# Loading two weights ahead of the second batch's raw keys, five conversion steps moved ahead, and the last key-pooling products later, in a pooled-attention and FFN kernel

## The chip, the cores and the metric

The kernel runs on one core of one Trainium2 chip. The metric is the device time of one execution in microseconds (us), the median of several runs; lower is better. The engines are named as the profile names them: PE is TensorE (PEld its weight loads, which overlap PE), DVE is VectorE, ACT is ScalarE, POOL is GpSimd, and SPq is the queue on SyncE that issues transfers.

## The reference

Keys and values are averaged over groups of 8 positions (576 positions become 72), attention runs on those, and its result is the input of a feed-forward network (FFN) with a leaky ReLU. The two weight matrices are float64 arrays, the rest is float32.

```python
B, H, S, D = q.shape                      # 8, 8, 576, 64; pool = 8, scale = 1/8
k_p = k.reshape(B, H, 72, 8, D).mean(axis=3)
v_p = v.reshape(B, H, 72, 8, D).mean(axis=3)
attn = softmax(scale * q @ k_p.T)         # 576 x 72 for each batch and head
x = (attn @ v_p).transpose(0, 2, 1, 3).reshape(4608, 512)
h = x @ w_in                              # 512 -> 2048
out = maximum(0.01 * h, h) @ w_out        # 2048 -> 512
```

## The kernel before

**The FFN** takes x in chunks of 512 tokens, transposed. Its products are made of three matmuls each: a value is split into a high and a low part of a rounded type (`xh` and `xl`, `gh` and `gl`, the two halves of a weight tile `w`), and high times high, high times low and low times high are added up in PSUM. A weight tile is a slice f of 128 of the 2048 hidden columns: `w_in` slice f and `w_out` slice f, 16 of each. `ph` (lines L944 to L946) is the first layer's product of a slice, ACT applies the leaky ReLU (L949) and makes `gh` (L952), DVE makes `gl` (L954), and `acc` (L969 to L971) is the second layer's product.

**The weights** arrive as float64 (512 KB a slice; `stage`, loads at L180 and L184) and are converted on the chip, once. A head of a conversion is two ACT instructions on the raw bits (L202, L203) and three of DVE (L206, L207, L210); its tail is the high part on ACT (L214) and the low part on DVE (L215). The steps are taken in one sequence: head of `w_in` 0, head of `w_in` 1, tail of `w_in` 0, head of `w_out` 0, tail of `w_in` 1, head of `w_in` 2, tail of `w_out` 0, head of `w_out` 1, and so on. `convert_to(n)` takes steps until n are taken; while chunk 0 is multiplied, it is called with 7 + 4f ahead of slice f.

**The attention** of batch 0 runs before the first FFN product, that of batch 1 between the products of chunk 0. Its units are named in `FIRST`: `q` transposes queries (L463, copied to `qT` at L465), `sa`/`sb` make the scores `pss` of four heads (L488), take the row maximum on DVE (L496) and the exponentials `e` on ACT (L500); `au` divides by the sum (`red`, L520, L521) and spreads the result into `at` (L534, L538; on DVE for row tiles 2 and 3 of batch 0, on POOL otherwise); `pu` transposes `at` into `pp` (PE, L591), from which ACT and DVE make `pT_hi`, `pT_rem` (L593, L594, L602), and multiplies it with the values into `pa` (PE, L619, L624); ACT and DVE turn `pa` into `xh` (L636) and `xl` (L637), which frees its bank. In `1kp0` to `1kp3` PE pools the raw keys of batch 1: eight products of `k0raw` ... `k3raw` with the identity each, summed in one bank `pk` (L301). `1kd` moves `pk` into `kT` (L308 on ACT, L309 on DVE). A `c` in `FIRST` is one conversion step.

**What sets the order.** PE runs in exactly the written order, that of `FIRST` and then of the loops. The order on ACT and DVE is set by the scheduler that builds the kernel; it keeps each engine's queue in one fixed order, and an instruction whose input is late holds those behind it. SPq issues the transfers in the order in which they are written. PSUM's banks are handed out in turn: from batch 1 on, attention uses two banks, so `pq` of a row tile needs the bank of a `pa` that `xl` has to have read.

Of the kernel before, what the change touches and what calls it, by code (L numbers as in the profile page):

```python
# [24 lines left out]
def tile_pooled_attention_ffn(  # L25
# [9 lines left out]
    nc = tc.nc  # L35
# [3 lines left out]
    POOL = 8  # L39
    SP = S // POOL  # L40
# [3 lines left out]
    NK = DM // P  # L44
# [18 lines left out]
    ]  # L63
    FIRST = (
# [99 lines left out]
    def spare(f, i, shape, dtype, name):  # L164

        return wts.tile(shape, dtype, tag=f"w{i}_{f}", name=name)

    def stage(f):

        if f >= NF:  # L170
            return
        slot = NF - 1 if f == NF - 2 else NF - 1 - f % SPARE
        for i in range(2):
            shape = [P, DM, 2]
            if slot > f:
                t = spare(slot, i, shape, I32, f"w{i}_bits{f}")
            else:
                t = two.tile(shape, I32, tag="raw", name=f"w{i}_bits{f}")
            if i == 0:
                nc.sync.dma_start(  # L180
                    t.rearrange("p (k f) w -> p k f w", k=NK), w_in[:, :, f * P : (f + 1) * P, :]
                )
            else:
                nc.sync.dma_start(t, w_out[:, f, :, :])  # L184
            bits[i, f] = t

    def convert(i, f):
# [70 lines left out]
    def raw_tile(b, nm):  # L258
        shape = [P, 2, POOL * D]
        if (b, nm) in RAW:  # L260
            return spare(*RAW[b, nm], shape, F32, f"{nm}raw{b}")
        return two.tile(shape, F32, tag="raw", name=f"{nm}raw{b}")
# [21 lines left out]
            )  # L284
        return raw

    def load_pairs(b):

        raws = []
        for p in range(NK):  # L290
            raws.append(raw_tile(b, f"k{p}"))
            raws[p] = raws[p][:SP].rearrange("s x y -> s (x y)").rearrange("s (a i d) -> s a i d", a=POOL, i=2)
            for i in range(2):
                nc.sync.dma_start(
                    raws[p][:, :, i, :], k[b, 2 * p + i].rearrange("(s a) d -> s a d", a=POOL)
                )
        return raws

    def pool_pair(pk, p, raw):
        for a in range(POOL):  # L300
# [375 lines left out]
    def attention(b):  # L676

        st = {}
# [12 lines left out]
            start_v()  # L691
            q_of[b, 3] = load_q(b, 3)

        def keys():
            st["pairs"] = load_pairs(b)

        def values():
            start, st["v"] = load_v(b)
# [91 lines left out]
        def pm(j, g):  # L790
# [3 lines left out]

        return {
            "loads": loads, "keys": keys, "values": values, "lk": lk, "lv": lv, "kd": kd,
            **{f"kp{p}": kp(p) for p in range(NK)}, "ku": ku, "vu": vu, "vp": vp,
            **{f"q{t}": qu(t) for t in range(len(where))},
# [236 lines left out]

    att = [attention(b) for b in range(B)]
    att[0]["loads"]()
    att[1]["keys"]()
    for f in range(SPARE):
        stage(f)  # L1040

    for u in FIRST.split():
        if u == "c":
# [10 lines left out]
    for b in range(2, B):  # L1054
        for j, piece in enumerate(PIECES[b]):
            c = 2 + (2 * TAIL + S * (b - 2) + piece[0][0]) // CH
# [86 lines left out]
```

## Time and profile before

| | us |
|---|---|
| median of 3 runs | 940.96 (940.75 to 941.16) |
| the profiled execution | 941.63 |
| its span | 939.7 |
| PE busy in the span | 907.3 |
| ACT busy | 411.8 |
| DVE busy | 392.3 |
| POOL busy | 176.1 |

The span is what the profiler saw of the program, the time of the execution is 1.9 us longer. Busy times overlap between engines. What PE is not busy, 32.4 us, is the time in which it waits for another engine or a transfer; instructions that run while PE is busy cost nothing of their own.

### The profile page before, as it was taken

The numbers are of one execution on the slowest core, as the hardware profiler recorded it, in microseconds if no ns is written. First come the engines' busy times: TensorE is split into PE (matmuls) and PEld (weight loads), VectorE is DVE, ScalarE is ACT, GpSimd is POOL, SyncE is SP. The second block draws the span as 40 slices with busy tenths as digits, with TensorE's granted clock in tenths as the row PEclk, the third lists the DMA queues.
The fourth block names the chain that finished last, engine by engine and source line by source line (L and its number), as shares of the span: only waits on it lengthen the run. The fifth ranks groups of instructions, "written<-read, shape, count | busy, mean of one in ns | idle before, by whom it ended". The sixth has DMA issues, their size and how long they took to land.

```text
span 939.7 us, 12662 instructions
## 1 busy us (share of the span) xinstructions
PE 907.3 (97%) x4293; PEld 755.8 (80%) x4293; DVE 392.3 (42%) x910; ACT 411.8 (44%) x1304; POOL 176.1 (19%) x329
## 2 busy tenths in 40 slices
PE   4998999999999989999999999999999999999998
PEld 3876788878888868888888888888888888888886
DVE  5799675524343233343244434353335322221111
ACT  4797764535343324343344435443535334223112
POOL 3012110231036520232023112230102001000000
PEclk9899999999999999999999999999999999999999
DMA  9996331242134560753076505840463122101001
GB/s 173 282 241 208 85 93 51 50 112 63 29 91 112 118 112 18 133 83 82 10 124 104 95 22 110 121 73 7 94 86 52 17 62 43 26 1 46 0 1 46
DMA packets 243257, 77.00 MB, mean 82 GB/s; under 512 B 217528, under 2 KB 226744, under 8 KB 243192
## 3 DMA queue, kind: packets, MB, share of 16 engines
q1 hardware_dynamic: 242616, 75.66, 37.6%
q8 instruction: 34, 0.56, 0.2%
q10 hardware_dynamic: 576, 0.52, 0.2%
q14 instruction: 31, 0.25, 0.1%
HBM read 56.56 MB, written 19.60 MB: 81 GB/s over the span
## 4 chain that ended last, share of the span: by engine, by line
PE 78%; DMA 6%; ACT 5%; DVE 3%; SPq 3%; POOL 3%; issue 1%; ACTq 0%; DVEq 0%; POOLq 0%
PE ph L944 12%; PE acc L969 12%; PE ph L946 12%; PE ph L945 12%; PE acc L971 12%; PE acc L970 11%; PE pss L488 3%; SPq L279 2%; DMA vremraw<-in_v_dram 1%; DMA k1raw<-in_k_dram 1%; PE pa L619 1%; ACT e L500 1%; DMA v1raw<-in_v_dram 1%; PE pa L624 1%; ACT w_bits L202 1%
## 5 line engine op out<-in xcount | busy, mean ns | idle before, releaser
L944 PE MATMUL ph<-xh,w 128*128 128x512 f32 x576 | 231.5, 402 | 0.5 <-DVE gl L954 0.5
L969 PE MATMUL acc<-w,gh 128*128 128x512 f32 x576 | 230.3, 400 | 0.0
L946 PE MATMUL ph<-xh,w 128*128 128x512 f32 x576 | 226.0, 392 | 0.6 <-DVE w L215 0.6
L945 PE MATMUL ph<-xl,w 128*128 128x512 f32 x576 | 225.9, 392 | 0.0
L971 PE MATMUL acc<-w,gl 128*128 128x512 f32 x576 | 225.2, 391 | 0.0
L970 PE MATMUL acc<-w,gh 128*128 128x512 f32 x576 | 224.7, 390 | 0.0
L954 DVE TENSOR_TENSOR gl<-ph,gh 128x512 fp32r<-128x512 f32 x144 | 99.0, 688 | 260.6 <-ACT gh L952 260.0
L949 ACT ACTIVATE ph<-ph 128x512 f32<-128x512 f32 x144 | 84.3, 586 | 265.0 <-PE ph L946 265.0
L500 ACT ACTIVATE e<-pss,red 128x72 f32<-128x72 f32 x320 | 98.2, 322 | 94.2 <-DVE red L496 79.8
L946 PEld LDWEIGHTS ph<-xh,w 128*128 128x128 f32 x576 | 108.7, 189 | 24.7 <-DVE w L215 1.0
L971 PEld LDWEIGHTS acc<-w,gl 128*128 128x128 f32 x576 | 108.2, 188 | 23.5
L944 PEld LDWEIGHTS ph<-xh,w 128*128 128x128 f32 x576 | 108.8, 189 | 21.3 <-DVE gl L954 0.9
L945 PEld LDWEIGHTS ph<-xl,w 128*128 128x128 f32 x576 | 108.9, 189 | 20.7 <-DVE xl L637 0.5
L969 PEld LDWEIGHTS acc<-w,gh 128*128 128x128 f32 x576 | 108.3, 188 | 20.8 <-DVE o L1003 0.4
L970 PEld LDWEIGHTS acc<-w,gh 128*128 128x128 f32 x576 | 108.5, 188 | 20.5
L528 POOL TENSOR_TENSOR at<-e,red 128x128 f32<-128x128 f32 x100 | 39.6, 416 | 276.3 <-DVE red L521 103.0
L952 ACT CAST gh<-ph 128x512 fp32r<-128x512 f32 x144 | 84.8, 589 | 3.7
L500 ACT ACTIVATION_READ_ACCUMULATOR e<-pss,red 128x1 f32 x320 | 66.2, 207 | 0.0
L496 DVE TENSOR_REDUCE red<-pss 128x4 f32<-128x288 f32 x80 | 36.2, 453 | 69.2 <-PE pss L488 69.0
L488 PEld LDWEIGHTS pss<-kT,qT 128*128 128x128 f32 x280 | 43.2, 189 | 9.4 <-ACT e L500 2.3
L488 PE MATMUL pss<-kT,qT 128*128 128x144 f32 x280 | 46.0, 286 | 2.6 <-ACT e L500 1.6
L534 POOL TENSOR_TENSOR blocks<-e,red 128x256 f32<-128x256 f32 x24 | 17.6, 732 | 144.6 <-DVE red L521 97.5
(143 smaller groups left out, 805.3 us busy)
## 6 DMA issues: line engine op xcount, KB each, us to landing
w_bits<-in_moe_w_in_dram SPq DMA_DIRECT2D x16, 512.0 KB
w_bits<-in_moe_w_out_dram SPq DMA_DIRECT2D x16, 512.0 KB
out_dram<-o SPq DMA_DIRECT2D x31, 256.0 KB
rows<-at SPq DMA_DIRECT2D x40, 192.0 KB
blocks<-rows SPq DMA_DIRECT2D x40, 120.0 KB
v0raw<-in_v_dram SPq DMA_DIRECT2D x16, 256.0 KB
v1raw<-in_v_dram SPq DMA_DIRECT2D x16, 256.0 KB
blocks<-rows SPq DMA_DIRECT2D x40, 96.0 KB
```

Of the source, the lines that this page charges most:

```text
L488: nc.tensor.matmul(sc[:, 2 * SP * i : 2 * SP * (i + 1)], qT[:, p, :], kT[:, p, :, :].rearrange("d i s -> d (i s)"), start=True, stop=True,)
L500: ins = nc.scalar.activation(e[:, h, :], scv[:, h, :], AF.Exp, bias=mx[:, h : h + 1], accum_out=sm[:, h : h + 1],)
L528: eng.tensor_tensor(cols[:, :, i, :].rearrange("a (h w) y -> a h w y", h=2), e[:, 2 * i : 2 * i + 2, 0:MAIN].rearrange("a h (w y) -> a h w ...
L944: nc.tensor.matmul(ph, w[:, 0, ks], xh[kk], start=kk == 0, stop=False)
L945: nc.tensor.matmul(ph, w[:, 0, ks], xl[kk], start=False, stop=False)
L946: nc.tensor.matmul(ph, w[:, 1, ks], xh[kk], start=False, stop=kk == NK - 1)
L949: nc.scalar.activation(ph, ph, AF.Prelu, alpha=0.01)
L952: casts.append(nc.scalar.copy(gh, ph))
L954: anchor["gl"] = nc.vector.tensor_tensor(gl, ph, gh.bitcast(F32), op=ALU.subtract)
L969: nc.tensor.matmul(a, gh[:, r], hi, start=first, stop=False)
L970: nc.tensor.matmul(a, gh[:, r], lo, start=False, stop=False)
L971: nc.tensor.matmul(a, gl[:, r], hi, start=False, stop=last)
```

## The change

The raw keys' loading is split by pair. The first slice of `w_in` is now issued ahead of the raw keys of batch 1 and the second between the two halves of these keys; the two first slices of `w_out` follow the keys. In `FIRST`, one `c` stands ahead of `au00`, two behind `sa30`, one behind `au01` and the rest late; there are eight in place of seven. `1kp2` moves behind `pu30 pu31`, and `1kp3` from there to behind `au11`, just ahead of `1kd`. The number of instructions on each engine stays the same. In the changed kernel the lines below L297 have numbers that are 4 smaller (L637 becomes L633).

```diff
     FIRST = (
         "k0 q0 sa00 k1 q1 sa01 sa10 sb00 q2 sb01 sa11 lv sb10 sb11 sa20 vu sa21 pu00 pu10 vp q3 "
-        "pu01 pu11 sb20 sb21 au00 sa30 sa31 au01 1kp0 c pu20 pu21 1kp1 sb30 sb31 1kp2 pu30 pu31 1kp3 1kd "
-        "c c au10 c au11 c c c"
+        "pu01 pu11 sb20 sb21 c au00 sa30 c c sa31 au01 1kp0 c pu20 pu21 1kp1 sb30 sb31 pu30 pu31 "
+        "1kp2 c au10 c au11 1kp3 1kd c c"
     )
...
-    def stage(f):
+    def stage(f, which=range(2)):
...
-        for i in range(2):
+        for i in which:
...
-    def load_pairs(b):
-
-        raws = []
-        for p in range(NK):
...
+    def load_pair(b, p):
+
+        raw = raw_tile(b, f"k{p}")
...
+        for i in range(2):
+            nc.sync.dma_start(raw[:, :, i, :], k[b, 2 * p + i].rearrange("(s a) d -> s a d", a=POOL))
+        return raw
...
-        def keys():
-            st["pairs"] = load_pairs(b)
+        def keys(*pairs):
+            st.setdefault("pairs", []).extend(load_pair(b, p) for p in pairs)
...
     att[0]["loads"]()
-    att[1]["keys"]()
+    stage(0, [0])
+    att[1]["keys"](0, 1)
+    stage(1, [0])
+    att[1]["keys"](2, 3)
     for f in range(SPARE):
-        stage(f)
+        stage(f, [1] if f < 2 else [0, 1])
```

PE's order at the end of batch 0's attention, where `pp_3_0` and `pp_3_1` are the transposes of the last row tile `at_3`. Before:

```order
L301 MATMUL pk_426<-ident,k1raw_166 128x72 x8
L301 MATMUL pk_426<-ident,k2raw_169 128x72 x8
L591 MATMUL pp_3_0_483<-ident,at_3_468 128x128 x3
L591 MATMUL pp_3_1_490<-ident,at_3_468 128x128 x3
L301 MATMUL pk_426<-ident,k3raw_172 128x72 x8
```

The same place in the changed kernel:

```order
L297 MATMUL pk_442<-ident,k1raw_168 128x72 x8
L587 MATMUL pp_3_0_491<-ident,at_3_484 128x128 x3
L587 MATMUL pp_3_1_498<-ident,at_3_484 128x128 x3
L297 MATMUL pk_442<-ident,k2raw_173 128x72 x8
L615 MATMUL pa_1_0_515<-pT_whole,v_first 128x256
...
L297 MATMUL pk_442<-ident,k3raw_176 128x72 x8
L940 MATMUL ph_0_576<-xh_0_389,w_0_379 128x512
```

The products of `k2raw` stood ahead of the two transposes of `at_3` and now stand behind them; those of `k3raw`, which followed the transposes, now come just ahead of the first FFN product.

DVE's order up to the last instruction that makes `at_3`. Before, from the second `xl` of batch 0 on:

```order
L637 TENSOR_TENSOR xl_1_387<-pa_0_1_392,xh_1_383 128x256
L496 TENSOR_REDUCE red_3_0_401<-pss_3_0_397 128x4
L496 TENSOR_REDUCE red_3_1_410<-pss_3_1_407 128x4
L520 TENSOR_TENSOR red_3_0_401<-red_3_0_401,tiny 128x4
L521 RECIPROCAL red_3_0_401<-red_3_0_401 128x4
L534 TENSOR_TENSOR at_3_468<-e_3_400,red_3_0_401 128x256
L538 TENSOR_TENSOR at_3_468<-e_3_400,red_3_0_401 128x128
L520 TENSOR_TENSOR red_3_1_410<-red_3_1_410,tiny 128x4
L521 RECIPROCAL red_3_1_410<-red_3_1_410 128x4
L637 TENSOR_TENSOR xl_2_388<-pa_0_2_416,xh_2_384 128x256
L534 TENSOR_TENSOR at_3_468<-e_3_400,red_3_1_410 128x256
L538 TENSOR_TENSOR at_3_468<-e_3_400,red_3_1_410 128x128
```

In the changed kernel, from just ahead of the first `xl` (`w_bits` are raw weights, `w_t` the one that is being converted):

```order
L206 TENSOR_SCALAR w_t_380<-w_bits_163 128x512
L207 SCALAR_TENSOR_TENSOR w_t_380<-w_bits_163,w_t_380 128x512
L633 TENSOR_TENSOR xl_0_393<-pa_0_0_386,xh_0_389 128x256
L210 ISA w_t_380<-w_bits_163,w_t_380 128x1024
L633 TENSOR_TENSOR xl_1_394<-pa_0_1_399,xh_1_390 128x256
L492 TENSOR_REDUCE red_3_0_408<-pss_3_0_404 128x4
L206 TENSOR_SCALAR w_t_415<-w_bits_171 128x512
L492 TENSOR_REDUCE red_3_1_426<-pss_3_1_423 128x4
L215 TENSOR_TENSOR w_0_379<-w_t_380,w_0_379 128x512
L633 TENSOR_TENSOR xl_2_395<-pa_0_2_432,xh_2_391 128x256
L207 SCALAR_TENSOR_TENSOR w_t_415<-w_bits_171,w_t_415 128x512
L516 TENSOR_TENSOR red_3_0_408<-red_3_0_408,tiny 128x4
```

Four rows later it goes on, to the last instruction of `at_3`:

```order
L207 SCALAR_TENSOR_TENSOR w_t_452<-w_bits_179,w_t_452 128x512
L530 TENSOR_TENSOR at_3_484<-e_3_407,red_3_0_408 128x256
L534 TENSOR_TENSOR at_3_484<-e_3_407,red_3_0_408 128x128
L516 TENSOR_TENSOR red_3_1_426<-red_3_1_426,tiny 128x4
L210 ISA w_t_452<-w_bits_179,w_t_452 128x1024
L598 SCALAR_TENSOR_TENSOR pT_rem<-pp_2_0_458,marks,pT_rem 128x128
L598 SCALAR_TENSOR_TENSOR pT_rem_1_1_466<-pp_2_1_467,marks,pT_rem_1_1_466 128x128
L517 RECIPROCAL red_3_1_426<-red_3_1_426 128x4
L215 TENSOR_TENSOR w_1_414<-w_t_415,w_1_414 128x512
L598 SCALAR_TENSOR_TENSOR pT_rem<-pp_3_0_491,marks,pT_rem 128x128
L530 TENSOR_TENSOR at_3_484<-e_3_407,red_3_1_426 128x256
L534 TENSOR_TENSOR at_3_484<-e_3_407,red_3_1_426 128x128
```

All conversion work stood behind `at_3` before. Now eleven instructions of conversions stand ahead of the last row (three each of L206, L207 and L210, two of L215, two of them in the four rows between, which also hold the fourth `xl` and a reciprocal), and three of L602 (now L598), which stood behind it as well.

ACT's order at the first leaky ReLU of the FFN (`ph_0`) up to the first exponentials of batch 1. Before:

```order
L214 CAST w_0_526<-w_t_527 128x512
L949 ACTIVATE ph_0_569<-ph_0_569 128x512
L952 CAST gh_0_592<-ph_0_569 128x512
L202 ACTIVATE w_bits_181<-w_bits_181 128x512
L203 ACTIVATE w_bits_181<-w_bits_181 128x512
L202 ACTIVATE w_bits_187<-w_bits_187 128x512
L203 ACTIVATE w_bits_187<-w_bits_187 128x512
L500 ACTIVATE e_0_0_599,red_0_0_600<-pss_0_0_596,red_0_0_600 128x72 x4
```

In the changed kernel:

```order
L461 COPY qT_0_588<-pq_0_583 128x512
L214 CAST w_1_558<-w_t_559 128x512
L945 ACTIVATE ph_0_576<-ph_0_576 128x512
L948 CAST gh_0_599<-ph_0_576 128x512
L202 ACTIVATE w_bits_187<-w_bits_187 128x512
L203 ACTIVATE w_bits_187<-w_bits_187 128x512
L496 ACTIVATE e_0_0_606,red_0_0_607<-pss_0_0_603,red_0_0_607 128x72 x4
```

One pair of conversion instructions in place of two stands between `gh_0` and the exponentials, and ahead of `ph_0` stands the tail of `w_out` 1 (`w_1`) where that of `w_out` 0 stood.

DVE's order at the third `xl` of batch 1's first piece, some 40 us later. Before:

```order
L215 TENSOR_TENSOR w_7_951<-w_t_952,w_7_951 128x512
L637 TENSOR_TENSOR xl_2_916<-pa_0_2_989,xh_2_912 128x256
L954 TENSOR_TENSOR gl_5_986<-ph_5_964,gh_5_985 128x512
L206 TENSOR_SCALAR w_t_1035<-w_bits_689 128x512
L207 SCALAR_TENSOR_TENSOR w_t_1035<-w_bits_689,w_t_1035 128x512
L206 TENSOR_SCALAR w_t_1044<-w_bits_866 128x512
L210 ISA w_t_1035<-w_bits_689,w_t_1035 128x1024
L207 SCALAR_TENSOR_TENSOR w_t_1044<-w_bits_866,w_t_1044 128x512
L637 TENSOR_TENSOR xl_3_917<-pa_0_3_994,xh_3_913 128x256
```

In the changed kernel:

```order
L215 TENSOR_TENSOR w_7_951<-w_t_952,w_7_951 128x512
L950 TENSOR_TENSOR gl_5_986<-ph_5_964,gh_5_985 128x512
L206 TENSOR_SCALAR w_t_1035<-w_bits_689 128x512
L207 SCALAR_TENSOR_TENSOR w_t_1035<-w_bits_689,w_t_1035 128x512
L206 TENSOR_SCALAR w_t_1044<-w_bits_866 128x512
L210 ISA w_t_1035<-w_bits_689,w_t_1035 128x1024
L207 SCALAR_TENSOR_TENSOR w_t_1044<-w_bits_866,w_t_1044 128x512
L633 TENSOR_TENSOR xl_2_916<-pa_0_2_989,xh_2_912 128x256
L633 TENSOR_TENSOR xl_3_917<-pa_0_3_994,xh_3_913 128x256
```

`xl_2` stood ahead of `gl_5` and now stands behind it and behind five conversion instructions, directly ahead of `xl_3`.

## Rows read from the trace of the kernel before

**Rows 1.** The page's first part: each engine's busy time, its share of the span and its instructions.

```profile
PE 907.3 (97%) x4293; PEld 755.8 (80%) x4293; DVE 392.3 (42%) x910; ACT 411.8 (44%) x1304; POOL 176.1 (19%) x329
```

**Rows 2.** Two stretches of the span: their length, busy time and instructions of PE, PEld, DVE, ACT and POOL, PE's granted clock (1.00 is 2.4 GHz, 0.50 is 1.2 GHz), the share of the DMA engines' time, GB/s.

```profile
40.00:60.00 20.00, 18.05 (x89) 14.52 (x89) 18.59 (x40) 19.37 (x53) 1.26 (x2) 0.91 1.05 256
...
360.00:900.00 540.00, 540.00 (x2524) 451.82 (x2523) 188.85 (x427) 207.62 (x663) 87.90 (x182) 1.00 0.34 61
```

**Rows 3.** PE in order of time from the end of batch 0's attention to the first scores of batch 1: start, duration, line, tiles, and in brackets the idle time ahead of it, where there is some.

```profile
35.32 1.90 PE L301 MATMUL pk<-ident,k1raw 72*128 72x72 f32 x16
37.06 1.95 PE L301 MATMUL pk<-ident,k2raw 72*128 72x72 f32 x16
...
38.85 0.82 PE L591 MATMUL pp<-ident,at 128*128 128x128 f32 x6
...
41.25 0.64 PE L619 MATMUL pa<-pT_whole,v_first 128*128 128x256 f32 x2
...
43.50 0.40 PE L944 MATMUL ph<-xh,w 128*128 128x512 f32 x1
...
46.98 0.65 PE L488 MATMUL pss<-kT,qT 128*128 128x144 f32 x4
```

**Rows 4.** DVE in order of time: the last instruction of `at_3` and what follows, and two rows of later conversions.

```profile
35.83 0.28 DVE L538 TENSOR_TENSOR at<-e,red 128x128 f32<-128x128 f32 x1
36.03 0.42 DVE L637 TENSOR_TENSOR xl<-pa,xh 128x256 fp32r<-128x256 f32 x1
36.36 0.42 DVE L206 TENSOR_SCALAR w_t<-w_bits 128x512 int32<-128x512 int32 x1
36.82 0.69 DVE L207 SCALAR_TENSOR_TENSOR w_t<-w_bits,w_t 128x512 int32<-128x512 int32 x1
37.42 0.60 DVE L602 SCALAR_TENSOR_TENSOR pT_rem<-pp,marks,pT_rem 128x128 fp32r<-128x128 f32 x2
...
48.32 0.67 DVE L215 TENSOR_TENSOR w<-w_t,w 128x512 fp32r<-128x512 f32 x1
48.92 0.68 DVE L210 CUSTOM_DVE_ANT_0 w_t<-w_bits,w_t 128x1024 uint16<-128x1024 uint16 x1
```

**Rows 5.** The stretch from the last L602 of row tiles 0 and 1 to the end of `at_3`; columns as in rows 2.

```profile
30.06:36.11 6.05, 6.05 (x48) 5.83 (x48) 3.73 (x15) 4.52 (x22) 0.00 (x0) 0.95 1.03 369
```

**Rows 6.** ACT in order of time: an exponential, the first conversion's two instructions, and the first L214 behind the FFN's start.

```profile
34.42 0.35 ACT L500 ACTIVATE e<-pss,red 128x72 f32<-128x72 f32 x1
...
35.23 0.73 ACT L202 ACTIVATE w_bits<-w_bits 128x512 f32<-128x512 f32 x1
35.81 0.70 ACT L203 ACTIVATE w_bits<-w_bits 128x512 int32<-128x512 uint32 x1
...
44.27 0.62 ACT L214 CAST w<-w_t 128x512 fp32r<-128x512 f32 x1
```

**Rows 7.** PE's waits behind the first FFN product: rows of PE that have idle time ahead of them, and the instruction that ended it.

```profile
52.23 0.76 PE L488 MATMUL pss<-kT,qT 128*128 128x144 f32 x4 [1.39 <-ACT e L500]
...
54.03 0.50 PE L946 MATMUL ph<-xh,w 128*128 128x512 f32 x1 [0.56 <-DVE w L215]
...
80.11 0.55 PE L591 MATMUL pp<-ident,blocks 128*128 128x128 f32 x3 [2.01 <-DVE xl L637]
...
89.33 0.76 PE L488 MATMUL pss<-kT,qT 128*128 128x144 f32 x4 [0.53 <-ACT qT L465]
...
340.53 0.42 PE L619 MATMUL pa<-pT_hi,v_hi 128*128 128x320 f32 x1 [2.84 <-ACT pT_hi L574]
```

**Rows 8.** Three stretches that follow waits of PE; columns as in rows 2.

```profile
55.00:58.00 3.00, 3.00 (x8) 2.32 (x7) 2.75 (x6) 3.00 (x10) 0.83 (x2) 0.51 1.07 344
80.00:84.00 4.00, 3.89 (x20) 3.12 (x20) 4.00 (x9) 1.97 (x6) 3.02 (x2) 1.00 0.65 167
341.00:345.00 4.00, 3.27 (x11) 3.04 (x12) 2.72 (x5) 1.76 (x4) 0.00 (x0) 0.57 0.47 75
```

**Rows 9.** Packets of all transfers in 22 to 26, 26 to 30 and 30 to 34 us.

```profile
DMA packets 2502, 0.64 MB, mean 159 GB/s; under 512 B 2501, under 2 KB 2501, under 8 KB 2501
...
DMA packets 1575, 1.05 MB, mean 264 GB/s; under 512 B 1003, under 2 KB 1504, under 8 KB 1574
...
DMA packets 895, 1.43 MB, mean 358 GB/s; under 512 B 45, under 2 KB 712, under 8 KB 895
```

**Rows 10.** ACT in order of time around 85 us.

```profile
85.43 0.37 ACT L636 CAST xh<-pa 128x256 fp32r<-128x256 f32 x1
85.69 0.58 ACT L952 CAST gh<-ph 128x512 fp32r<-128x512 f32 x1
```

**Rows 11.** DVE in order of time around 85 to 90 us.

```profile
85.04 0.69 DVE L215 TENSOR_TENSOR w<-w_t,w 128x512 fp32r<-128x512 f32 x1 [0.42 <-ACT w L214]
85.83 0.42 DVE L637 TENSOR_TENSOR xl<-pa,xh 128x256 fp32r<-128x256 f32 x1
86.31 0.69 DVE L954 TENSOR_TENSOR gl<-ph,gh 128x512 fp32r<-128x512 f32 x1
...
88.95 0.68 DVE L207 SCALAR_TENSOR_TENSOR w_t<-w_bits,w_t 128x512 int32<-128x512 int32 x1
89.56 0.41 DVE L637 TENSOR_TENSOR xl<-pa,xh 128x256 fp32r<-128x256 f32 x1
```

**Rows 12.** PE: the transposes of the fourth query tile of batch 1.

```profile
86.81 0.60 PE L463 MATMUL pq<-ident,q 128*128 128x128 f32 x4
```

More of the change, by code (lines that the diff above doesn't have):

```diff
@@ L285, in load_main @@
         return raw
-    def load_pairs(b):
-        raws = []
-        for p in range(NK):
[L291 to L297, printed above, removed]
+    def load_pair(b, p):
+        raw = raw_tile(b, f"k{p}")
+        raw = raw[:SP].rearrange("s x y -> s (x y)").rearrange("s (a i d) -> s a i d", a=POOL, i=2)
+        for i in range(2):
+            nc.sync.dma_start(raw[:, :, i, :], k[b, 2 * p + i].rearrange("(s a) d -> s a d", a=POOL))
+        return raw
     def pool_pair(pk, p, raw):
```

## The prediction

> **What bounds the kernel now.** I read the page's busy times first, then stretches, then PE in order of time where a stretch is not full. PE is busy for 907.3 of 939.7 us [rows 1], and from 360 to 900 us for every one of 540 [rows 2], so a microsecond that PE loses or wins ahead of that is one at the end. It can be won only where PE waits. The stretch from 40 to 60 us, where the first FFN products run beside the weights' conversion, shows who makes it wait: PE is busy for 18.05 of 20 us, but DVE for 18.59 and ACT for 19.37 [rows 2]. In this start the conversion's engines are full, and work put ahead of something that PE needs delays it by its own length. The profiled execution took 941.63 us, 1.93 around its span of 939.70 and 0.67 above the median of 940.96; I add the sum to 941.63 and take 0.67 off. About 0.2%, 1.9 us, is what a measurement of this kernel can tell from no change.
>
> **First place: `at_3`.** Before, PE pools `k2raw` from 37.06 us and comes to the transposes of `at_3` at 38.85 [rows 3]; DVE had finished `at_3` at 36.11 (35.83 + 0.28) [rows 4], so nothing waits. In the new order both sides move the wrong way. PE no longer has `k2raw` there, so it asks for `at_3` at 37.06. DVE has eleven conversion instructions, three of L602 and one more `xl` ahead of it. Price of each, from one start to the next: L206 0.34 (its 0.42 less the 0.08 by which rows overlap), L207 0.60 (36.82 to 37.42), L215 0.60 (48.32 to 48.92), L210 as long as L215 in duration, so 0.60, L602 0.26 (two within a row of 0.60, less the overlap), `xl` 0.33 (36.03 to 36.36) [rows 4]. Sum: 3 x 0.34 + 3 x 0.60 + 3 x 0.60 + 2 x 0.60 + 3 x 0.26 + 0.33 = 6.93. DVE was busy for 3.73 of the 6.05 us up to 36.11 [rows 5], so at most 2.32 go into its idle time; at least 4.61 are left, and `at_3` is done at about 40.7. The second transpose group could start 0.35 behind 37.06, at 37.41; PE loses 3.3 us, in two waits. Bounds: 2.5, if some of these instructions are ordered more kindly by the time the exponentials arrive, and 4.6, if DVE can't fill its idle time because it waits for ACT. ACT itself has some 3.8 us more ahead of the last exponentials of `at_3` (three pairs L202 and L203 at 1.15, one L214), which come about 2.3 later with its own idle time of 1.5 [rows 5, 6]: due before DVE is there, so not a second price.
>
> **The clock behind it.** After waits of 1.39 and 0.56 with little work between [rows 7], the granted clock was at 0.51 from 55 to 58 us; after the wait of 2.84 it was 0.57 on the mean from 341 to 345; after the single wait of 2.01 at 80.11 it stayed 1.00 [rows 7, 8]. Half clock is 1.2 GHz, so a stretch of about 3.4 us at it costs 1.7. Two waits that add up to 3.3 within some 4 us are more than the case at 52 to 54, so I take 1.6, bounds 0 and 1.7. The Trainium skill (TensorE: Matmul & The Clock Gate, Part 1: The HAM clock gate) says that "the default state is throttled, and activity releases the throttle"; by that alone every such wait would cost its half clock, the second place below too, and the sum would be +5.9 in place of the +5.3 I come to; the wait at 80.11 disagrees, and the sum without any clock term is +2.5. The first FFN product comes at 43.50 + 3.3 + 1.6 = 48.4.
>
> **What is given back.** Conversions done early are not there later. PE's waits at 52.23 (1.39, for exponentials on ACT) and 54.03 (0.56, for a weight's low part on DVE) and the half clock behind them (1.7) are 3.65 us [rows 7]. The 0.56 goes, since the step that it waits for comes earlier. Of the 1.39, a pair L202 and L203 (1.15) leaves ACT's queue ahead of the exponentials, but the L214 ahead of `ph_0` now waits for a DVE that is itself behind by the first place; about one DVE instruction of that, 0.6, comes back. I keep 0.85 as wait, and with no second wait beside it no half clock: -2.8, bounds -3.65 and -1.1 (half clock stays).
>
> **Second place: `xl_2`.** PE's `pq` at 86.81 us ran without a wait [rows 12]: `xl_2`, which frees its bank, had run at 85.83 [rows 11]. In the new order `xh_2` on ACT stands behind `gh_5` and two pairs L202 and L203, and `xl_2` on DVE behind `gl_5` and five conversion instructions, where `xl_3` stood. On ACT: 85.43, one 0.5 and two times 1.15, so `xh_2` starts at 88.2 [rows 6, 10]. On DVE: `xl_3` started at 89.56, less the 0.48 that `xl_2` took ahead of it (85.83 to 86.31) and up to 0.3 by the earlier `gh_5`, so `xl_2` ends at 89.2 to 89.5 [rows 11]. `pq` at 86.81 then waits 2.5 us, bounds 0 (if PE arrives late here) and 2.8. The wait of 0.53 for `qT` at 89.33 [rows 7] goes, since ACT has time for it behind `pq`: together +2.0. The wait lies between the 2.01 that had no half clock and the 2.84 that had, nearer to the latter: 1.2, bounds 0 and 1.7.
>
> **What costs nothing.** Loads: before, the raw keys' small packets are 2501 of 2502 in 22 to 26 us, 1003 of 1575 in the next 4 us and 45 of 895 after that, so the keys are in by about 30 [rows 9]. Two slices of 512 KB ahead of or among them are 1.05 MB; at 264 to 358 GB/s they push the keys back by 2.9 to 4.0 us, to 33 or 34. `k2raw` is needed at 41. `w_in` 0, now first, is needed by ACT at about 29.6. The one at risk is `w_out` 0 behind the keys: 0.52 MB at 358 GB/s more, so in at 34 to 35.5, needed by ACT near 35 (35.23, plus two pairs and an L214, less four exponentials at 0.3, less ACT's idle 1.5 [rows 5, 6]); the price is the rival below. `kT`, whose last products come later: PE has from 41.25 to 46.98 and the 1.74 of `k3raw` (35.32 to 37.06), 7.5 us, between the first `pa` and the scores that need it [rows 3]; DVE's work in between is ten instructions, 4.8 us, and one hand-over of about 1. Hidden, by some 1.5; without that cover it costs its excess, up to 1. The waits from 58 to 85 us, with 2.01 as the largest [rows 7], keep their order: 0, bounds -2.0 and +1.
>
> **Sum:** 3.3 + 1.6 - 2.8 + 2.0 + 1.2 = +5.3. 941.63 + 5.3 = 946.9 for the profiled execution, 946.3 by the median.
>
> **The rivals.**
> - *Only the first place costs.* PE comes to `pq` late anyway, or `xl_2` is not waited for. Then 3.3 + 1.6 - 2.8 - 0.5 = +1.6: 942.6. For it speaks that all shown times shift; against it that ACT and DVE shift with PE there, as they are fed by its products.
> - *The other side: `at_3` isn't late.* The conversions fit into DVE's idle time and only the gains are left: -3.65, 937.3. It decides at the 1.3 us between 36.11 and 37.41: DVE would have to take the 6.93 us with its 2.32 idle and 1.3 of slack, so at half their price. The rows of DVE don't show any such price.
> - *`w_out` 0 lands late.* ACT holds its L202 and behind it the exponentials for `at_3`'s second half; DVE holds its L206, which stands ahead of the first half. From about 35 on each microsecond late adds one; 2 to 4 late gives 948.5 to 950.5. For it: all of DMA is busy then; against: the two halves of the keys need not be in for it.
> - *No change.* The clock stays up after the first waits and the second place is hidden: 3.3 - 2.8 - 0.5 = 0: 941.0.
>
> **How the numbers follow.** The forecast, both places cost, has 0.70 and its own range is 944.6 to 948.6 (no clock term in the second place with a little less in the first; the upper bounds of the clock and 4.0 at the first). Only the first place 0.08, the other side 0.07, `w_out` 0 late 0.10, no change 0.05. The range from 943.0 to 949.4 leaves out the two last on the low side, the one at 942.6 and half of the late landing, about 0.2 with the forecast's own tails. Faster by over 0.2% is the other side, 0.07; within 0.2% are no change and the better half of the first rival, 0.10; slower 0.83.
>
> **What would show it.** In the profile after: PE's row of `pp` behind `k1raw` with idle time of 0.7 and again 2.4 us, put down to DVE L534; a granted clock near 0.5 behind it; the first FFN product at about 48.4; no wait of 0.56 at `w` L215; and a wait of about 2.5 us ahead of the fourth `pq`, put down to DVE `xl` L633, near 89 us. PE's busy time would grow by half-clock stretches, the rest of the trace be shifted. The prediction is wrong if `at_3` ends ahead of 38 us, if the conversions wait for their weights, or if the fourth `pq` has no idle time ahead of it.

## The result, and the profile after

The changed kernel takes 949.13 us (median of 7 runs, 945.86 to 950.06); the kernel before took 941.16 in the same comparison. The medians lie 8.0 apart; the ratio that goes with the 95% interval is 1.0065 (1.0049 to 1.0081): 6.1 us slower, between 4.6 and 7.6. The profiled execution is the fastest of the seven, 945.86 us with a span of 944.1, 4.4 more than before.

The page of the changed kernel, busy times. PE executes as many products as before [rows 1] and is busy for 2.4 us longer and idle for 2.0 longer (34.4 in place of 32.4), so the time is waiting and clock.

```profile
PE 909.7 (96%) x4293; PEld 757.8 (80%) x4293; DVE 392.2 (42%) x910; ACT 412.5 (44%) x1304; POOL 174.2 (18%) x329
```

PE of the changed kernel in order of time, from the pooling of `k1raw` to the first FFN product (start, duration, line, tiles, idle time ahead and what ended it):

```profile
36.32 1.90 PE L297 MATMUL pk<-ident,k1raw 72*128 72x72 f32 x16
...
38.06 0.52 PE L587 MATMUL pp<-ident,at 128*128 128x128 f32 x3
...
40.77 0.52 PE L587 MATMUL pp<-ident,at 128*128 128x128 f32 x3 [2.19 <-DVE at L530]
...
48.48 0.48 PE L940 MATMUL ph<-xh,w 128*128 128x512 f32 x1
```

The first transposes of `at_3` follow `k1raw` at once, the second ones wait 2.19 us, where before both ran without a wait [rows 3]. DVE at the same time, from the end of the first half of `at_3` to the end of the second:

```profile
37.90 0.28 DVE L534 TENSOR_TENSOR at<-e,red 128x128 f32<-128x128 f32 x1
...
38.17 0.68 DVE L210 CUSTOM_DVE_ANT_0 w_t<-w_bits,w_t 128x1024 uint16<-128x1024 uint16 x1
...
38.77 0.60 DVE L598 SCALAR_TENSOR_TENSOR pT_rem<-pp,marks,pT_rem 128x128 fp32r<-128x128 f32 x2
...
40.22 0.41 DVE L530 TENSOR_TENSOR at<-e,red 128x256 f32<-128x256 f32 x1
...
40.55 0.28 DVE L534 TENSOR_TENSOR at<-e,red 128x128 f32<-128x128 f32 x1
```

DVE does conversions and L598 between the two halves of `at_3` without a gap, and is done at 40.83, where it was at 36.11 before [rows 4]. What PE waits for is DVE's order, not an input. Then the clock, in stretches (columns as in rows 2), with PE's wait ahead of the last one:

```profile
42.70:46.00 3.30, 3.30 (x12) 2.85 (x11) 0.47 (x2) 0.82 (x3) 0.00 (x0) 0.50 0.86 206
...
92.00:96.00 4.00, 4.00 (x22) 3.42 (x22) 2.09 (x5) 2.43 (x10) 0.00 (x0) 1.00 0.85 277
...
344.59 0.64 PE L615 MATMUL pa<-pT_hi,v_hi 128*128 128x320 f32 x1 [3.68 <-ACT pT_hi L570]
...
343.00:350.00 7.00, 4.85 (x14) 4.09 (x15) 4.71 (x9) 3.01 (x6) 0.00 (x0) 0.51 0.46 73
```

Behind the second transposes the clock is at half up to 46 us, and behind the fourth `pq` (92 to 96) at full. It is at half again from 343 to 350 us, twice as long as behind the same wait before [rows 8]. The waits of PE that the prediction named, up to the scores behind the fourth `pq`:

```profile
55.99 0.76 PE L484 MATMUL pss<-kT,qT 128*128 128x144 f32 x4 [0.35 <-ACT e L496]
...
82.11 0.55 PE L587 MATMUL pp<-ident,blocks 128*128 128x128 f32 x3 [2.00 <-DVE xl L633]
...
91.32 0.66 PE L459 MATMUL pq<-ident,q 128*128 128x128 f32 x4 [2.32 <-DVE xl L633]
...
93.20 0.65 PE L484 MATMUL pss<-kT,qT 128*128 128x144 f32 x4
```

The wait of 1.39 at the second scores is 0.35 now and that of 0.56 is gone; at the fourth `pq` there is a new one of 2.32, ended by `xl` [rows 7, 12]. DVE there:

```profile
87.65 0.68 DVE L950 TENSOR_TENSOR gl<-ph,gh 128x512 fp32r<-128x512 f32 x1
...
90.85 0.74 DVE L633 TENSOR_TENSOR xl<-pa,xh 128x256 fp32r<-128x256 f32 x2
```

`xl_2` runs as the first of the two at 90.85, behind `gl` and the five conversion instructions that start at 88.25 to 90.25, where before it ran ahead of them [rows 11].

With these rows the 4.4 us of this trace can be split at four points that both traces have: `k1raw`, the first FFN product, the `pp` behind the wait of 2.0, and the scores behind the fourth `pq` (35.32, 43.50, 80.11 and 89.33 before [rows 3, 7]); 0.35 is what the second transposes need behind the first ones without a wait:

| part | forecast | this trace |
|---|---|---|
| up to `k1raw` (36.32 - 35.32) | 0 | +1.0 |
| first place, waiting (40.77 - 38.06 - 0.35) | +3.3 | +2.4 |
| the clock behind it ((48.48 - 36.32) - (43.50 - 35.32) - 2.36) | +1.6 | +1.6 |
| given back ((82.11 - 48.48) - (80.11 - 43.50)) | -2.8 | -3.0 |
| second place ((93.20 - 82.11) - (89.33 - 80.11)) | +2.0 | +1.9 |
| the clock behind it | +1.2 | 0 |
| from there to the end | 0 | +0.5 |
| sum | +5.3 | +4.4 |

The last row hides two larger terms. From the scores at 93.20 PE's lag falls from 3.9 to 2.8 us up to matching products at 309.95 (307.16 before); what gives this back stays open. Then it rises to 4.6 at 392.97 (388.37 before), behind a wait that is 0.8 longer than before [rows 7] and the longer half clock at 343 to 350 us, a place that the forecast does not name.

The other executions are up to 4 us longer. Each comes with its granted clock and span, and (1 - clock) x span is an estimate of what the clock took, an upper one, as half clock costs nothing while PE waits: on the mean of 12 runs of the changed kernel 10.8 us, of the 82 runs of before beside e1 to e12 7.3. The means are 948.4 and 942.2 us: of these 6.2 us, 3.5 are clock and 2.7 are everything else. In the profiled execution the clock took 8.5 (0.991 of 944.1).

### The profile page after: what moved, and what is told of

Same layout as the page of the kernel before. It is cut to its first block, busy times and chain, and to the rows that moved or that the text cites. A ratio compares the mean times of both kernels' runs of the same rounds, so it can differ in the third digit from the quotient of the medians.

```text
span 944.1 us, 12665 instructions
## 1 busy us (share of the span) xinstructions
PE 909.7 (96%) x4293; PEld 757.8 (80%) x4293; DVE 392.2 (42%) x910; ACT 412.5 (44%) x1304; POOL 174.2 (18%) x329
## 4 chain that ended last, share of the span: by engine, by line
PE 77%; DMA 7%; ACT 4%; DVE 4%; POOL 3%; SPq 3%; issue 1%; ACTq 0%; DVEq 0%; POOLq 0%
PE ph L940 12%; PE acc L965 12%; PE acc L967 12%; PE ph L942 12%; PE ph L941 12%; PE acc L966 11%; PE pss L484 3%; DMA vremraw<-in_v_dram 2%; SPq L279 1%; DMA k1raw<-in_k_dram 1%; ACT e L496 1%; PE pa L615 1%; DMA v0raw<-in_v_dram 1%; PE pa L620 1%; PE pa L618 1%
## 5 line engine op out<-in xcount | busy, mean ns | idle before, releaser
L633 DVE TENSOR_TENSOR xl<-pa,xh 128x256 fp32r<-128x256 f32 (+4 forms) x68 | 27.5, 406 | 43.6 <-ACT xh L632 42.5
```

## The experiments

The theory: PE waits at `at_3` and at the fourth `pq` because DVE has conversion steps ahead of what PE needs, and some of these waits are followed by half clock. The rivals: the order of the loads does it; the lost cover of `k2raw` on PE does it; early steps are a loss as such.

**e1: the loads alone.** The changed order of loads, the units of before.

```diff
-        "pu01 pu11 sb20 sb21 c au00 sa30 c c sa31 au01 1kp0 c pu20 pu21 1kp1 sb30 sb31 pu30 pu31 "
-        "1kp2 c au10 c au11 1kp3 1kd c c"
+        "pu01 pu11 sb20 sb21 au00 sa30 sa31 au01 1kp0 c pu20 pu21 1kp1 sb30 sb31 1kp2 pu30 pu31 1kp3 1kd "
+        "c c au10 c au11 c c c"
```

> The changed kernel's order of loads (first w_in slice ahead of the raw keys, second between their halves), but the order of units of the kernel before. Theory (the time is lost on DVE, ahead of at_3 and of xl_2): same as before within 1.5 us, no wait at the transposes of at_3 behind k1raw or k2raw, waits of about 1.4 and 0.6 at 52 to 54 us as before. Rival (the loads do it: keys pushed back, or the start slowed): 4 to 7 us slower than before, with PE waiting for raw keys ahead of 44 us.

Measured: 942.18 us against 942.00, ratio 1.0005 (0.9992 to 1.0018). PE's waits in order of time:

```profile
52.29 0.76 PE L484 MATMUL pss<-kT,qT 128*128 128x144 f32 x4 [1.40 <-ACT e L496]
...
54.06 0.50 PE L942 MATMUL ph<-xh,w 128*128 128x512 f32 x1 [0.55 <-DVE w L215]
```

They are those of before, and there is none at `at_3`. The loads are not the cause; a loss of up to 1.7 us is not excluded by the interval (e12 comes back to it).

**e2: the units alone.** The changed `FIRST`, the loads in the order of before (all raw keys, then the weights).

```diff
-    stage(0, [0])
-    att[1]["keys"](0, 1)
-    stage(1, [0])
-    att[1]["keys"](2, 3)
+    att[1]["keys"](0, 1, 2, 3)
     for f in range(SPARE):
-        stage(f, [1] if f < 2 else [0, 1])
+        stage(f)
```

> The loads in the order of the kernel before, the units in the changed order. Theory: 4.5 to 7 us slower than before; the wait at at_3 behind k1raw is there (2.2 us or more in all; up to 1 more, if the first slice of w_in, now behind the keys, comes after 30 us and holds the first conversion on ACT), and the wait of about 2.3 at the fourth pq of batch 1. Rival (the loads do it): within 1.5 us of before.

Measured: ratio 1.0063 (1.0043 to 1.0084), 5.9 us slower. One row of ACT, and PE:

```profile
30.52 0.67 ACT L202 ACTIVATE w_bits<-w_bits 128x512 f32<-128x512 f32 x1 [0.92 <-DMA w_bits<-in_moe_w_in_dram]
...
38.29 0.55 PE L587 MATMUL pp<-ident,at 128*128 128x128 f32 x3 [1.34 <-DVE at L530]
...
39.65 0.52 PE L587 MATMUL pp<-ident,at 128*128 128x128 f32 x3 [0.81 <-DVE at L530]
...
92.00 1.11 PE L459 MATMUL pq<-ident,q 128*128 128x128 f32 x4 [2.35 <-DVE xl L633]
```

Both places are there with 2.15 and 2.35 us of waiting, so the order of units makes them. The first is not quite that of the changed kernel: with the old order of loads ACT waits 0.92 us for the first slice of `w_in` and 1.00 for the second (at 33.29), which delays the conversions, and an `xl` stands between the two halves of `at_3` on DVE. Behind the second place the clock was at half this time:

```profile
92.00:96.00 4.00, 4.00 (x16) 3.45 (x17) 2.17 (x4) 1.10 (x2) 0.00 (x0) 0.62 0.79 234
```

**e3: PE kept busy at `at_3`.** The products of `k1raw` once more in front of the transposes.

```diff
-... 1kp1 sb30 sb31 pu30 pu31 "
+... 1kp1 sb30 sb31 1kp1 pu30 pu31 "
```

> The changed kernel with eight products more on PE: the pooling of k1raw is done a second time, with the same result, just ahead of the transposes of at_3, where PE would wait. DVE's order up to the last row of at_3 stays that of the changed kernel. Theory: at_3 is done at the same time, about 40.8 us, so PE waits some 1.7 us less, and works as much more, without loss; with PE busy there the granted clock stays at 1.00 from 41 to 46 us, and the first FFN product comes 1.5 to 2 us earlier than in the changed kernel (48.5), at about 46.7. That is the price of the half clock alone. Rival (the clock costs nothing of its own): first FFN product at 48.3 to 48.7. The order at xl_2 falls back to that of before in this build, so the wait of 2.3 at the fourth pq should be gone as well: 0 to 2 us slower than before in all.

Measured: ratio 1.0042 (1.0026 to 1.0058), 4.0 us slower. PE and the clock:

```profile
40.42 0.88 PE L587 MATMUL pp<-ident,at 128*128 128x128 f32 x3 [1.30 <-DVE at L530]
...
49.65 0.47 PE L940 MATMUL ph<-xh,w 128*128 128x512 f32 x1
```

```profile
40.50:47.00 6.50, 6.50 (x26) 6.12 (x27) 1.61 (x4) 1.03 (x4) 0.00 (x0) 0.50 0.90 189
```

Half of what was expected came: the wait fell by 0.9, to 1.30, and the one at the fourth `pq` is gone, as the order there fell back to that of before. The other half is the start: the products of `k1raw` began at 35.10, 1.2 us earlier than in the changed kernel's trace, and `at_3` was done only 0.4 earlier, at 40.47. But the clock went to half all the same, for twice as long as in the changed kernel's trace, and the first FFN product came at 49.65. What a half-clock stretch costs alone was not settled by this run, and that keeping PE busier would avoid it was wrong.

**e4: `xl_2` ahead of the conversions.**

```diff
-                if b == 0:
+                if b < 2:
                     anchor["act"], anchor["dve"] = cast, ins
```

> The changed kernel with one rule more for the order: conversion heads written behind an xl of batch 1 stay behind it on DVE too. Up to 60 us the order is that of the changed kernel; at the second place xl_2 stands ahead of the five conversion instructions again, though behind gl_5. Theory: the wait at at_3 (2.2 us) and the first FFN product (48.5 us) stay, the wait at the fourth pq falls from 2.3 to between 0.5 and 1.7 us, and the time to 1 to 3 us below the changed kernel's, 2 to 5 above before. Rival (the wait at pq is not made by xl_2's place behind the conversions): the wait stays at 2.3, no gain.

Measured: ratio 1.0064 (1.0041 to 1.0088). DVE, and PE behind it:

```profile
90.31 0.68 DVE L950 TENSOR_TENSOR gl<-ph,gh 128x512 fp32r<-128x512 f32 x1
...
92.02 0.42 DVE L633 TENSOR_TENSOR xl<-pa,xh 128x256 fp32r<-128x256 f32 x1 [1.03 <-ACT xh L632]
```

```profile
38.90 0.55 PE L587 MATMUL pp<-ident,at 128*128 128x128 f32 x3 [1.02 <-DVE at L530]
...
41.65 0.87 PE L587 MATMUL pp<-ident,at 128*128 128x128 f32 x3 [2.19 <-DVE at L530]
...
92.50 0.66 PE L459 MATMUL pq<-ident,q 128*128 128x128 f32 x4 [0.93 <-DVE xl L633]
```

The wait at the fourth `pq` fell from 2.32 to 0.93, so `xl_2`'s place behind the conversions on DVE makes 1.39 of it; in what is left `xl_2` itself waits 1.03 us for ACT's `xh`. The rule holds for every `xl` of batch 1, and the wait of 2.0 at 80 us changes, too (1.12 here). The time does not follow as clearly: the median, 947.32, is 1.8 below the changed kernel's, but the ratio to before is the same, so the gain in time is not shown. In this trace the first transposes of `at_3` wait, too, 1.02 us, and half clock there lasted from 41 to 51 us, three times as long as in the two traces of the changed kernel (6.8 us in e2 and e3):

```profile
41.00:51.00 10.00, 9.35 (x37) 8.66 (x37) 4.39 (x11) 3.44 (x9) 0.00 (x0) 0.50 1.08 211
```

**e5: PE's units alone.** Kernel before, with only `1kp2` and `1kp3` moved.

```diff
-"... 1kp1 sb30 sb31 1kp2 pu30 pu31 1kp3 1kd c c au10 c au11 c c c"
+"... 1kp1 sb30 sb31 pu30 pu31 1kp2 c c au10 c au11 1kp3 1kd c c c"
```

> Only PE's units moved: the pooling of k2raw behind the transposes of at_3 and that of k3raw ahead of 1kd behind au11, loads and the other conversion steps as before. Theory: DVE still finishes at_3 at about 36.1 us, PE comes to it at about 37.1, so no wait there; within 1.5 us of before. Rival (the cover of k2raw is what was lost): a wait of 1 us or more at the transposes of at_3, 1.5 to 4 us slower.

Measured: ratio 0.9986 (0.9972 to 0.9999), 1.3 us faster if anything. PE:

```profile
36.77 0.82 PE L591 MATMUL pp<-ident,at 128*128 128x128 f32 x6
...
43.13 0.47 PE L944 MATMUL ph<-xh,w 128*128 128x512 f32 x1
```

All six transposes of `at_3` run behind `k1raw` without a wait. Moving `k2raw` away costs nothing while DVE is in time.

**e6: `k2raw`'s cover back.** The changed kernel, with `1kp2` ahead of `pu30 pu31`.

```diff
-"... 1kp1 sb30 sb31 pu30 pu31 1kp2 c au10 c au11 1kp3 1kd c c"
+"... 1kp1 sb30 sb31 1kp2 pu30 pu31 c au10 c au11 1kp3 1kd c c"
```

> The changed kernel with the pooling of k2raw ahead of the transposes of at_3 again, as before; k3raw stays late, the steps stay early. Theory: at_3 is done at the same 40.8 us, PE has 1.7 us of work more ahead of it, so the wait is 1.2 to 1.7 in place of 2.9, the clock stays up, and the first FFN product comes at about 45.3 in place of 48.5 (1.7 less waiting, 1.6 less half clock). What was won later stays won, and the order at xl_2 falls back to that of before in this build: 1.5 us faster to 1 slower than before. Rival (the steps' early place costs their whole length whatever PE does): first FFN product at 46.8 or later and 2 to 4 us slower than before.

Measured: ratio 1.0002 (0.9992 to 1.0012). PE:

```profile
40.69 0.52 PE L587 MATMUL pp<-ident,at 128*128 128x128 f32 x3 [0.55 <-ACT pT_whole L589]
...
45.24 0.47 PE L940 MATMUL ph<-xh,w 128*128 128x512 f32 x1
```

The wait shrinks to 0.55, put down to ACT now, and the first FFN product comes at 45.24, as expected. e5 and e6 together: the products' move alone makes no wait, and the steps' early place alone makes little (the first FFN product comes 11.52 us behind the start of `k0raw`'s products, 33.72, against 10.57 before); it takes both, the steps ahead of `at_3` and the products behind it, to make the whole of the first place.

**e7: three steps spread, `k2raw` and `k3raw` as before.**

```diff
+"pu01 pu11 sb20 sb21 c au00 sa30 sa31 au01 1kp0 c pu20 pu21 1kp1 sb30 sb31 1kp2 c pu30 pu31 1kp3 1kd "
+"c c au10 c au11 c c"
```

> Loads as in the changed kernel; only one conversion step ahead of au00, one behind 1kp0, and the third and later ones behind 1kp2 as DVE gets free; pooling of k2raw and k3raw where they were before. Eight steps in all. Theory: at_3 is in time, the first FFN product comes at 43 to 44 us as before, the waits at 52 to 54 us shrink from 1.9 to below 0.8 with no half clock behind them, so that PE is 2 to 3.5 us ahead of before at 65 us; at the fourth pq xl_2 stands behind the conversions as in the changed kernel and takes 2 to 2.8 of it back: 1.5 us faster to 2 us slower than before in all. Rival (early steps are themselves the loss): no lead at 65 us.

Measured: ratio 1.0048 (1.0029 to 1.0067), 4.5 us slower: a miss, expected was 1.5 faster to 2 slower. PE, and one row of ACT:

```profile
43.59 0.40 PE L940 MATMUL ph<-xh,w 128*128 128x512 f32 x1
...
51.33 0.76 PE L484 MATMUL pss<-kT,qT 128*128 128x144 f32 x4 [0.39 <-ACT e L496]
...
56.00 0.66 ACT L202 ACTIVATE w_bits<-w_bits 128x512 f32<-128x512 f32 x1 [1.60 <-DMA w_bits<-in_moe_w_in_dram]
...
58.51 0.52 PE L587 MATMUL pp<-ident,blocks 128*128 128x128 f32 x3 [1.78 <-issue]
...
88.81 1.11 PE L459 MATMUL pq<-ident,q 128*128 128x128 f32 x4 [2.33 <-DVE xl L633]
```

```profile
88.00:92.00 4.00, 3.19 (x10) 2.71 (x11) 2.98 (x6) 1.58 (x3) 0.00 (x0) 0.57 0.60 182
```

The first FFN product is as early as before (43.59), and the scores of 52.23 come at 51.33. But the lead, 3.3 us at 58 us, is spent in a wait of 1.78 at 58.51 and more of them up to 79.61 (2.03), and the second place, with half clock behind it, takes its part: at 101 us PE is 2.6 behind before. The wait at 58.51 is not made by the order alone: ACT, with the exponentials behind it, had waited 1.60 us for a slice of `w_in` to land (in e8, with the same units, 0.48, and PE's wait there is 0.72). An early step only helps if its weight is there and nothing behind it has slipped in the order. This trace is of the fastest of the five executions (941.30); it makes the 2.6 good by 388 us, in part as it has no half clock around 340 us, where that of before has 3.4 us. So it does not show the whole of the 4.5.

**e8: e7 with the later steps paced slower.**

```diff
-                convert_to(7 + 4 * f)
+                convert_to(7 + 4 * f + [0, 0, -1, -2, -2, -2, -1, -1][f])
```

> As the kernel with three early steps, with the later steps paced one or two later from the third FFN slice on (7 + 4f less 0, 0, 1, 2, 2, 2, 1, 1), which puts xl_2 ahead of the conversions again. Theory: the lead of 2 to 3.5 us at 65 us is kept at the fourth pq, where the wait is gone; 1.5 to 3.5 us faster than before. Rival: the lead is lost at another wait between 65 and 105 us, within 1 us of before.

Measured: ratio 0.9988 (0.9977 to 1.0000), 1.1 us faster, less than the 1.5 expected and not clear of no change. PE:

```profile
88.31 0.76 PE L484 MATMUL pss<-kT,qT 128*128 128x144 f32 x4 [1.33 <-ACT qT L461]
```

The scores of 89.33 come at 88.31 and the wait at `pq` is gone, though there is one of 1.33 for `qT` ahead of these scores. Against e7 only the pace of later steps has changed, and the median is 5.4 us lower. Of this the two traces show 3.6 at 101 us (0.9 ahead of before here, 2.6 behind it in e7): the second place, the clock behind it and the waits ahead of it. The rest is not shown.

**e9: the changed kernel again.**

> The changed kernel again, unaltered, for a second trace of it and more times. Its waits at at_3 (2 to 3 us) and at the fourth pq (2.3) are set by orders that don't vary, so they should come back. Theory: what varies is only whether a wait is followed by a half-clock stretch; if one follows the fourth pq this time, the trace from there to 105 us is 1.1 to 1.7 us longer than in the first one. Rival (some other wait varies): the waits themselves differ by over 1 us. Time: 946 to 950 us, 5 to 7 us above before.

Measured: 948.15 us, ratio 1.0068 (1.0054 to 1.0082); the trace's span is 947.4, 3.3 more than the first one's. PE, and one row of ACT:

```profile
41.73 0.52 PE L587 MATMUL pp<-ident,at 128*128 128x128 f32 x3 [2.19 <-DVE at L530]
...
83.27 0.55 PE L587 MATMUL pp<-ident,blocks 128*128 128x128 f32 x3 [2.02 <-DVE xl L633]
...
88.52 0.58 ACT L945 ACTIVATE ph<-ph 128x512 f32<-128x512 f32 x1 [1.48 <-PE ph L942]
...
93.94 0.66 PE L459 MATMUL pq<-ident,q 128*128 128x128 f32 x4 [2.98 <-DVE xl L633]
...
96.88 1.17 PE L484 MATMUL pss<-kT,qT 128*128 128x144 f32 x4
```

```profile
84.00:88.00 4.00, 4.00 (x14) 3.19 (x13) 3.77 (x8) 1.45 (x5) 2.36 (x2) 0.57 0.84 250
...
94.00:96.00 2.00, 2.00 (x8) 1.65 (x9) 1.64 (x4) 1.10 (x2) 0.00 (x0) 0.64 0.78 256
```

The waits of 2.19 and 2.0 are the same, that at `pq` is 2.98. What differs is half clock behind two of them, some 3.4 us each (84.32 to 87.74 and from 94.56): from the `pp` to the scores behind `pq` this trace takes 13.61 us (83.27 to 96.88), the first one 11.09 (82.11 to 93.20), 2.5 more. The expectation of 1.1 to 1.7 was for one such stretch. That the wait at `pq` grew by 0.66 is the slower PE ahead of what `xl_2` needs: ACT's leaky ReLU waits 1.48 us for PE's `ph` in place of 0.85, and the same conversions and `xl_2` follow it in the same order.

**e10 and e11: two versions on these lines.** Both with three steps early, five (e10) or six (e11) late, another pace, and `xl` of batch 1 ahead of the heads as in e4.

```diff
+# e10
+"pu01 pu11 sb20 sb21 c au00 sa30 sa31 au01 1kp0 c pu20 pu21 1kp1 sb30 sb31 c pu30 1kp2 pu31 1kp3 1kd "
+"c au10 c au11 c c c"
+                convert_to(7 + 4 * f + [-1, -1, -1, -1, -2, -3, -3, -1][f])
+# e11
+"... sb31 1kp2 c pu30 pu31 1kp3 1kd c au10 c c au11 c c c"
+                convert_to(7 + 4 * f + [0, 1, 1, 0, 1, 0, 0, 0][f])
```

> What the experiments so far point to: loads as in the changed kernel; one step ahead of au00, one behind 1kp0, one behind sb31, five behind 1kd; the later steps paced up to three later (7 + 4f less 1, 1, 1, 1, 2, 3, 3, 1); conversion heads behind xl of batch 1 stay behind it. Theory: at_3 in time, first FFN product as early as before (10.6 us behind the start of k0raw), no wait of 1.4 at 52 us, and no wait at the fourth pq: PE 2 to 4 us ahead of before at 105 us, and 1.5 to 4 us faster than before. Rival: the lead goes to other waits between 60 and 100 us: within 1 us of before.

> A second version on the same principle: steps ahead of au00, behind 1kp0, behind 1kp2, five behind 1kd (one between au10 and au11 more), the later ones paced 7 + 4f plus 0, 1, 1, 0, 1, 0, 0, 0; conversion heads behind xl of batch 1 stay behind it. Theory: waits of 1 to 1.7 us at 52 and 58 us stay, those at 80 us (2.0) and at the fourth pq are gone: 1.5 to 4 us faster than before. Rival: within 1 us of before.

Measured: e10 0.9986 (0.9969 to 1.0003), e11 0.9984 (0.9973 to 0.9994): 1.3 and 1.5 us faster, at the lower edge of what was expected; e10's interval reaches no change. In e10 the waits at `at_3` and at the fourth `pq` are gone; part of the gain went to half clock without a wait:

```profile
32.00:41.00 9.00, 9.00 (x81) 8.90 (x80) 8.09 (x24) 7.36 (x31) 0.00 (x0) 1.00 1.04 360
...
41.00:42.00 1.00, 1.00 (x9) 1.00 (x8) 0.89 (x3) 0.84 (x2) 0.00 (x0) 0.72 1.34 229
42.00:43.00 1.00, 1.00 (x4) 0.82 (x4) 0.84 (x2) 0.40 (x1) 0.00 (x0) 0.50 0.48 85
```

In e11 one wait for exponentials is longer than forecast, 3.68 in place of some 1.5, with a granted clock of 0.58 behind it (62 to 64 us). Ahead of these exponentials ACT had waited 2.45 us for a slice of `w_in`:

```profile
57.79 0.67 ACT L202 ACTIVATE w_bits<-w_bits 128x512 f32<-128x512 f32 x1 [2.45 <-DMA w_bits<-in_moe_w_in_dram]
...
62.50 0.88 PE L587 MATMUL pp<-ident,blocks 128*128 128x128 f32 x3 [3.68 <-ACT e L496]
```

**e12: e11 with the first load of `w_in` behind two of the raw keys.**

```diff
-    stage(0, [0])
     att[1]["keys"](0, 1)
+    stage(0, [0])
     stage(1, [0])
```

> The second tuned version with one move in the order of loads: the first slice of w_in behind the first two raw keys instead of ahead of them; the order on every engine is the same. It asks whether this load, ahead of the keys, delays what batch 0 still waits for. In the traces with the load ahead, DVE begins on the last values of batch 0 (vremraw) 9.1 to 9.6 us after their transfer is issued, in those with the old order 7.9 to 8.9. Theory (the load takes its transfer's time from them): 7.9 to 8.9 here, k0raw's products begin at 32.5 to 33.2 us, and the time is 0.3 to 1.2 us below the second tuned version's, 1.8 to 3.5 below before. Rival (only scatter of the start): 9.1 or more, or no gain beyond 0.3 us. The load itself has to land by about 29.6 us; if it comes later, the first conversion on ACT and DVE waits and takes the gain back.

Measured: ratio 0.9982 (0.9968 to 0.9996), 939.96 us, 1.7 below before: the lowest ratio of all, though not clear of e5, e8, e10 and e11, and faster than both kernels by its interval, though by less than the 0.2% set above. ACT has no wait for a weight here, and the wait of 3.68 in e11 is 1.20 (at 59.12). DVE's first instruction on `vremraw`, issued at 12.50:

```profile
21.14 0.43 DVE L267 TENSOR_TENSOR vremraw<-vremraw 128x256 f32<-128x256 f32 x1 [1.09 <-DMA vremraw<-in_v_dram]
```

That is 8.64 us after the issue. In the four traces where the load is not ahead of the keys it is 7.9 to 8.9 (mean 8.5), in the ten where it is 8.5 to 9.6 (mean 9.1). By these means the load costs batch 0's last values some 0.6 us, and with them part of the 1.0 ahead of `k1raw`. This is not shown: the groups overlap, the expectation's 9.1 to 9.6 is 8.5 to 9.6 over all ten, and a gain of this size against e11 (0.5 by the medians, 0.2 by the ratios) lies within the intervals.

## Why the prediction was right, point by point

**First place: mechanism right, waiting too large by 0.9.** `at_3` was forecast for 40.7 and came at 40.83. But PE was there at 38.06, not at 37.06, since everything ahead of it was 1.0 late, and of the two waits, 0.7 and 2.4, only the second came (e4 has both). DVE set when `at_3` was done, so PE's lateness only took the place of waiting: the first two rows of the table, 1.0 and 2.4, are together the 3.3 that were forecast. e5 and e6 show the two halves of the cause apart.

**The clock behind it: 1.6 forecast, 1.6 in the first trace.** As a rule it was less certain than it looked: e6 with 0.55 of waiting had none, e2 and e3 with 2.15 and 1.30 had twice the length, e4 three times.

**Given back: -2.8 forecast, -3.0 measured**, with 0.35 instead of 0.85 left at the second scores.

**Second place: +2.0 forecast, +1.9 measured**, wait 2.3 in place of 2.5. e4 shows that 1.39 of it is `xl_2`'s place on DVE; e2, e7 and e9 show that it comes back.

**The clock behind the second place: 1.2 was a mean of two cases.** The first trace has none of it, e2, e7 and e9 have a whole stretch. Over all runs the clock's share of the loss is 3.5 us, where the terms of the sum had 1.6 + 1.2 - 1.7 = 1.1; the share of everything else is 2.7 where they had 3.3 - 1.1 + 2.0 = 4.2. The two errors nearly cancel, which is why the sum, 5.3, came near the 6.1; that is luck. The prediction's +2.5 "without any clock term" still holds the 1.7 given back; without any clock its terms give 4.2. It also quotes the Trainium skill (TensorE: Matmul & The Clock Gate, Part 1: The HAM clock gate), that "the default state is throttled, and activity releases the throttle". That each wait would then cost its half clock is the prediction's own step and does not stand in that sentence; it gave +5.9, nearer to the 6.1, but the waits of 2.0 and 2.3 in the first trace had none behind them, so it is not borne out wait by wait. Two places were left out of the sum: the wait of 2.0 at 80 us, the same in both kernels, which was followed by half clock in e3, e6 and e9, and the one around 340 us, where half clock lasted 6.8 us in the first trace and 3.4 before (up to 1.7 us more, outside the forecast's terms).

**Loads costed at nothing: nearly so.** `w_out` 0 wasn't late, the rival on it fell. But the prediction priced only the transfers that moved back, not those already under way ahead of the one that moved forward (e12: some 0.6 us by the means, not shown).

The rival "only the first place" fell with the wait at `pq`, "the other side" with that at `at_3`. The range, 943.0 to 949.4, held the median, near its upper edge; the forecast was 2.8 us below it. That it held is luck in part: the median, 949.1, lies above the forecast's own range, up to 948.6 (its terms even give 947.6: 946.3 + 0.1 + 0.5 + 0.7), and the rest of the range was there for a late `w_out` 0, the rival that fell (2 to 4 us late would have been 948.3 to 950.3).

## What to carry to other kernels

Filler work that an engine does in a fixed order belongs behind the last instruction that another engine is about to wait for; count what stands ahead of that instruction, and compare with when the waiting engine comes, which a move on that side changes too. A scheduler that reorders by its own times can turn a move at one place into a wait some 50 us later, so read the new order for the whole stretch in which it differs. Work that is pulled forward also has to find its input there: in e7, e8 and e11 ACT waited 1.60, 0.48 and 2.45 us for a weight, and with 1.60 and 2.45 PE's lead went into waits for what stood behind it. One execution can't price a change here, as half clock at places that the change does not touch moves it by 1.7 us and more.

## What the runs showed of the hardware

Half clock (1.2 GHz) did not follow a fixed rule on the waits. The same wait of 2.0 us at 80 us was followed by a half-clock stretch in three traces (e3, e6, e9) and by none in six (before, the first after, e1, e2, e5, e7), in the changed kernel both ways (its two traces). In e10 the clock fell between 41 and 42 us with PE busy for all of the 9.00 us up to 41 (the rows of e10 above). In e4 half clock at the first place lasted 10 us in place of the usual 3.4, with PE busy from 41.65 on. Around 340 us every version waits for ACT's `pT_hi`, 1.55 to 4.29 us, and half clock there lasted 3.4 us in five traces (before, e2, e5, e9, e11), 6.8 in eight (the first after, e1, e3, e4, e6, e8, e10, e12) and was missing in e7, with the shortest wait. While PE is busy each of these stretches costs half its length, some 1.7 us for the usual 3.4. They account for much of what the executions of the changed kernel differ by, from 945.86 to 950.06 us: the clock took 8.5 us of the fastest and 13.3 (0.986) of the slowest, though one of 949.92 has 10.4 (0.989).
